# Recurrent scan and gated FFN on one core: one product for three parameters, one row spread earlier, and a new transfer order before the first down projection

## The chip, the cores and the metric

The kernel runs on one core of one Trainium2 chip. The metric is the device time of one execution in microseconds (us), as the median of repeated runs. In the profile, PE is TensorE (matmuls), PEld its weight loads, DVE is VectorE, ACT is ScalarE, POOL is GpSimd, and SP is SyncE, which issues nearly all transfers here. Times within an execution are counted from the start of the profiled span.

## What is computed

The input is x with 2048 positions of 512 features in bf16. It is normalised over the features, and two branches are built from the normalised xn:

```python
xn  = layernorm(x)
Bu  = xn @ B_bar.T                    # complex, B_bar = ((Lam_bar - 1) / Lam)[:, None] * B
h_t = Lam_bar * h_{t-1} + Bu_t        # complex, Lam_bar = exp(exp(log_dt) * Lam)
y   = 2 * real(h @ C.T) + xn * Dskip
g   = silu((gelu(xn @ w_gate) * (xn @ w_up)) @ w_down)
out = x + y * g
```

The parameters Lambda_re, Lambda_im and log_dt are vectors of 512; Dskip is a row of 512; B and C are complex 512 x 512; the FFN is 1376 wide.

## The kernel before

**Slabs.** The 2048 positions are worked in four slabs (0 to 3) of 512, each of four tiles `m` of 128 positions. For each slab, `gate_tile` (L519, products recorded at L530) multiplies the transposed xn with `w_gate` and `w_up`; ACT evicts the results as `gt` (gelu) and `ub` (L538, L546); DVE multiplies them into `at` (L548, L550); `at_t` (L553) turns `at` by a transposing transfer into `atT` (L556); `down_pair` (L563, matmuls at L573) multiplies it with `w_down` for two tiles, and ACT evicts silu as `g` (L577). Slab 0 uses `GatePair` (L479) in three column chunks instead (matmuls L501, evictions L513 for `ub` and L514 for `gt`, product L516), because weights and xn arrive piece by piece.

**Recurrence.** `inputs` (L628) forms B times xn for half of the state (L638, evicted as `U` at L641). `states` (L644) rotates it so that the complex recurrence becomes real scans: a product `Q` with the tables `tab` (L656), sums into `W` (L664), four scans into `Fs` (L675), a product `Q` again (L656) and sums into `hst` (L664). `y_tile` (L582, matmuls L601) multiplies `hst` with `C2` onto the skip term already in the bank; DVE multiplies with `g` (`yg`, L604), adds x (`ot`, L606), and the result is stored (L609).

**Preparation.** `columns` (L391) turns log_dt and Lambda_im from rows to columns by a matmul with an identity; `damping` (L736) does the same for Lambda_re in a second matmul (L739) with a copy (L740), and derives the damping `rho` on POOL. `head_t` (L744) transposes the centred x of slab 0 on PE (L445), and ACT or DVE evicts it (L448, L449). `spread` (L747) copies Dskip's row to all partitions with a one-row matmul (L748) and an eviction (L749). `tables` (L708) builds `tab` on DVE (L725). `coefficients` (L822) forms `cre`, `cim`, `ncre` in two groups of tiny DVE operations (L827 to L834, and L837 to L845). The transposed C (`CT`, which lies in the buffer `hst1`) becomes `C2` for each of four column groups: ACT forms `tF` (L897), and DVE forms two products from it (L899, L902). There is one `tF` buffer, so the next `tF` waits for both products of the one before.

**PSUM.** Three slots of two banks and two single banks. `slot()` hands the three slots round in turn; a product into a slot waits until ACT has evicted what was in it.

**What sets the order.** Every operation is added to a plan (`Plan`, L24) with an estimated cost, its reads and writes, and sometimes `after` (a forced predecessor), `rank` (a preference) or `not_before`. PE operations keep the order in which the code adds them; all other engines, and SP's queue of transfers, get the order that `run` (L154) finds by list scheduling and a random search. The order is fixed when the program is built. `dma_first` chains transfers on one queue. Slab 1's statistics and normalisation (`norm1`, L860) run on DVE; those of slabs 2 and 3 (`norm_act`, L871) load x and let ACT form sums by two passes over each tile (`junk`, L876).

Of the kernel before, what the change touches and what calls it, by code (L numbers as in the profile page):

```python
# [12 lines left out]
AF = mybir.ActivationFunctionType  # L13
# [189 lines left out]
def kernel(  # L203
# [17 lines left out]
    nc = tc.nc  # L221
    P = 128
# [27 lines left out]
    def sb(name, shape, dt=BF16):  # L250
        return consts.tile(shape, dt, name=name)
# [5 lines left out]
    wd = sb("wd", [P, NFT, D])  # L257
    BT = sb("BT", [P, 2, KT, D])
    C2 = sb("C2", [P, 2, NPT, D])
    pv = [sb("pv0", [2 * NPT, P]), sb("pv1", [NPT, P])]  # L260
    Drow = sb("Drow", [P, D])
    hst = [sb(f"hst{i}", [P, 2, NPT, TS]) for i in range(2)]
    CT = hst[1]
# [67 lines left out]
    def load_x(eng, q, m, land):  # L331
        dma_first(eng, 0.45, land, lambda: q.dma_start(out=x_tok[:, m, :], in_=x_r[:, m, :]), [("x", 0, m)], not_before=0.72)

    load_p(0, A_log_dt, pv[0][0:NPT, :])
    load_p(1, A_Lambda_im, pv[0][NPT : 2 * NPT, :])
    behind = [first[ACT]]
    load_p(2, A_Lambda_re, pv[1][:])
    dma(ACT, 0.4, 3.0, lambda: nc.scalar.dma_start(out=Drow[0:1, :], in_=A_Dskip.rearrange("(a d) -> a d", a=1)), writes=["Drow"], after=[first[ACT]], rank=-20.0)
    def load_first(c, which, land):
        load_w(dma_first, SP, nc.sync, c, (1.45 * (CH0[c][1] - CH0[c][0]) / 512, land), which)  # L340
# [10 lines left out]
    def load_rest():  # L351

        for ri, src in enumerate((A_B_re, A_B_im)):
            dma_first(SP, 1.9, 5.0, lambda ri=ri, src=src: nc.sync.dma_start_transpose(out=BT[:, ri, :, :], in_=src), [("BT", ri)])
        first[SP] = turn_slab(0, 3.5, [first[SP]])
        dma_first(SP, 1.45, 3.5, lambda: nc.sync.dma_start(out=x_tok[:, M : 2 * M, :], in_=x_r[:, M : 2 * M, :]), [("x", 1, m) for m in range(M)])
        for which in range(2):
            load_w(dma_first, SP, nc.sync, 2, (1.35, 3.5), which)
        load_c(0)

    def load_c(ri):
        dma_first(SP, 1.9, 4.0, lambda: nc.sync.dma_start_transpose(out=CT[:, ri, :, :], in_=(A_C_re, A_C_im)[ri]), [("CT", ri)])

    def turn_slab(s, land, after=()):

# [20 lines left out]
    acts(1, lambda: act(out=tiny[:], in_=zero[:], func=AF.Exp), ["zero"], ["tiny"], table="exp", rank=150.0, after=behind)  # L386
    pf = small("pf", 16)
    dt_, thn, lim, lre = (pf[:, 4 * i : 4 * i + 4] for i in range(4))
    rows = slots[2][:, 0, 0 : 2 * NPT]

    def columns():  # L391

        pe(1, 150, lambda: T.matmul(rows, lhsT=pv[0][:], rhs=ident[0 : 2 * NPT, 0 : 2 * NPT], start=True, stop=True),
            [("pv", 0), ("pv", 1), "ident"], [("slot", 2, 0)])
        acts(4, lambda: act(out=dt_, in_=rows[:, 0:NPT], func=AF.Exp), [("slot", 2, 0), "tiny"], ["dt"], table="exp", rank=150.0)

    def turn_angles():
        dve(4, lambda: V.tensor_copy(out=lim, in_=rows[:, NPT : 2 * NPT]), [("slot", 2, 0)], ["lim"], base=0.14)
        dve(4, lambda: V.tensor_tensor(out=thn, in0=lim, in1=dt_, op=ALU.mult), ["lim", "dt"], ["thn"])

    iota_i = sb("iota_i", [P, NBA], I32)
# [77 lines left out]
    class GatePair:  # L479
# [24 lines left out]
        def close(self):  # L504
            m, c, q, pss = self.m, self.c, self.q, self.pss
            a, b = CH0[c]
            w = b - a
            qb, qo = q // 2, (q % 2) * 512
            gd, ud = gt[qb][:, qo : qo + w], ub[qb][:, qo : qo + w]
            kw, rd, ptr = {}, [], 0  # L510
            if self.bare:
                kw, rd, ptr = dict(scale=rs[:, 0, m : m + 1]), [("rs", 0, m)], 1
            up = acts(w, lambda: act(out=ud, in_=pss[1][:, 0:w], func=AF.Copy, **kw), self.both + rd, [("ub", q)], ptr=ptr)  # L513
            gelu = acts(w, lambda: act(out=gd, in_=pss[0][:, 0:w], func=AF.Gelu_apprx_tanh, **kw), self.both + rd, [("gt", q)], table="gelu", ptr=ptr,  # L514
                 after=[*early, up] if c + m == 0 else (), rank=60.0 if c + m == 0 else 0.0)
            dve(w, lambda: V.tensor_tensor(out=at[m][:, a:b], in0=gd, in1=ud, op=ALU.mult), [("gt", q), ("ub", q)], [("at", m, c)], rate=2.0)  # L516
            return gelu

    def gate_tile(s, m):  # L519
# [24 lines left out]
        for kind, (nm, wt, dst) in enumerate((("wg", wg, gt[q]), ("wu", wu, ub[q]))):  # L544
# [5 lines left out]
        dve(b - a, lambda: V.tensor_tensor(out=at[j][:, a:b], in0=gt[q][:, a:b], in1=ub[q][:, a:b], op=ALU.mult),  # L550
            [("gtb", q), ("ubb", q)], [("at", j, 2)], rate=2.0)

    def at_t(s, m, c0, c1):  # L553
        j = (s * M + m) % NAT
        k0, k1 = CK[c0][0], CK[c1][1]
        dma(SP, 1.3, 2.2, lambda: nc.sync.dma_start_transpose(  # L556
            out=atT[:, k0:k1, m * P : (m + 1) * P], in_=at[j][:, k0 * P : k1 * P]),
            [("at", j, c) for c in range(c0, c1 + 1)] + [("atpad", j)], [("atT", m, c) for c in range(c0, c1 + 1)])

    g2s = {}  # L560
    g2_n = [0]
# [60 lines left out]
    def half(s, h):  # L622
        inputs(s, h)
        states(s, h)
# [76 lines left out]
        else:  # L701
            dve(196, lambda: V.scalar_tensor_tensor(out=kr[:], in0=ang[:], scalar=-1.0, in1=ang[:], op0=ALU.mult, op1=ALU.max), ["ang"], ["kr"], base=0.13)

    def sines():
        early.append(acts(196, lambda: act(out=sbt[:], in_=ang[:], func=AF.Sin, scale=TWO_PI), ["ang"], ["sbt"], table="silu", rank=20.0))
        early.append(acts(196, lambda: act(out=cbt[:], in_=kr[:], func=AF.Sin, scale=-TWO_PI, bias=halfpi[:]), ["kr", "halfpi"], ["cbt", "trig"], table="silu", rank=20.0))

    def tables(behind):  # L708
        NB4 = [P, NPT, NA, NB // 2, 2]
# [25 lines left out]

    def damping():  # L736

        ps = ybank[0][:, 0:NPT]
        pe(1, 150, lambda: T.matmul(ps, lhsT=pv[1][:], rhs=ident[0:NPT, 0:NPT], start=True, stop=True), [("pv", 2), "ident"], [("y", 0)])  # L739
        dve(4, lambda: V.tensor_copy(out=lre, in_=ps), [("y", 0)], ["lre"], base=0.14)  # L740
        dve(4, lambda: V.tensor_tensor(out=a1[:], in0=lre, in1=dt_, op=ALU.mult), ["lre", "dt"], ["a1"])
        power(rho[:], e_t[:], a1[:], 4, ["a1", "e_t"], ["rho"])

# [30 lines left out]
    norm_dve(0, 0)  # L774
    pl.in_turn = False
    head_t(0, ACT)
    dummies(2, 0)
    behind = [head_t(1, ACT)]
    acts(1, lambda: act(out=tiny[:], in_=zero[:], func=AF.Sin), ["zero", "dt"], ["tiny"], table="silu", rank=60.0, after=behind)
    sines()  # L780
    pairs = [GatePair(m, 0, m == M - 1) for m in range(M)]
    pairs[0].products(0)
    spread()
    pairs[1].products(0)
    pairs[0].products(1)
    head_t(2, ACT)
    pairs[1].products(1)
    damping()
    pairs[2].products(0)
    pl.in_turn = True  # L790
    head_t(3, DVE)
# [4 lines left out]
    pairs[2].products(1)  # L796
    pairs[3].products(0)
    pairs[3].products(1)
    gelus = [p.close() for p in pairs]
    tables(gelus[:1])  # L800
    load_rest()
# [2 lines left out]

    def gate_pairs(m, c):
        p = GatePair(m, c, (c, m) == (1, M - 1))
        p.products(0)
        p.products(1)
        p.close()

    for m in range(M):
        gate_pairs(m, 1)
    for h in range(2):
        half(0, h)
    for m in range(M):
        gate_pairs(m, 2)
        at_t(0, m, 0, 2)

    c1, s1 = cbt[:, :, 1], sbt[:, :, 1]
    cre, cim, ncre = small("cre"), small("cim"), small("ncre")  # L820
# [36 lines left out]
             [("x", s, m), ("rs", s, m), ("nb", s)], [("xn", m)], ptr=2)  # L857
        dma(SP, 1.2, 1.3, lambda: nc.sync.dma_start_transpose(out=xnT[s % 2][:, m, :, :], in_=xn[m]), [("xn", m)], [("xnT", s % 2, m)])

    def norm1():  # L860
        for m in range(M):
            stats(1, m)
            mean(1, m)
        rstd(1, 0, M)
        for m in range(M):
            norm_dve(1, m)
        first[SP] = turn_slab(1, 3.0, [first[SP]])
        for m in range(M):
            skip(1, m)

    def norm_act(s):  # L871
        dma(SP, 0.5, 4.0, lambda: nc.sync.dma_start(out=x_tok[:, s * M : (s + 1) * M, :], in_=x_r[:, s * M : (s + 1) * M, :]),
            writes=[("x", s, m) for m in range(M)], not_before=(30.0, 50.0)[s - 2], rank=40.0)
        for m in range(M):
            for i, fn in enumerate((AF.Copy, AF.Square)):
                acts(512, lambda i=i, fn=fn, m=m: act(out=junk[:], in_=x_tok[:, s * M + m, :], func=fn, accum_out=sx[:, s, i, m : m + 1]),  # L876
                     [("x", s, m)], ["junk", ("sx", s, i, m)], ptr=2)
        mean, var = sx[:, s, 0, :], sx[:, s, 1, :]

        def f():  # L880
            V.tensor_scalar(out=mean, in0=mean, scalar1=1.0 / D, scalar2=None, op0=ALU.mult)
            V.tensor_tensor(out=mq[:, s, :], in0=mean, in1=mean, op=ALU.mult)
            V.tensor_scalar(out=var, in0=var, scalar1=1.0 / D, scalar2=EPS, op0=ALU.mult, op1=ALU.add)
            V.tensor_tensor(out=var, in0=var, in1=mq[:, s, :], op=ALU.subtract)
        pl.add(DVE, 0.35, f, [("sx", s, i, m) for i in range(2) for m in range(M)], [("var", s)], lag=0.13)
        power(rs[:, s, :], var, mhalf[:], M, [("var", s), "mhalf"], [("rs", s, m) for m in range(M)])
        dve(M, lambda: V.scalar_tensor_tensor(out=nb[:, s, :], in0=mean, scalar=-1.0, in1=rs[:, s, :], op0=ALU.mult, op1=ALU.mult),
            [("var", s)] + [("rs", s, m) for m in range(M)], [("nb", s)])
        for m in range(M):
            norm_out(s, m)  # L890

    norm1()
    dma_first(SP, 3.6, 4.3, lambda: nc.sync.dma_start(out=wd[:, 0 : NFT - 1, :], in_=B_w_down[0 : (NFT - 1) * P, :].rearrange("(k p) d -> p k d", p=P)), ["wd"])
    dma_first(SP, 0.4, 4.3, lambda: nc.sync.dma_start(out=wd[:FL, NFT - 1, :], in_=B_w_down[(NFT - 1) * P : F, :]), ["wd"])
    load_c(1)
    for pt in range(NPT):
        acts(1024, lambda pt=pt: act(out=tF[:, :, :], in_=CT[:, :, pt, :], func=AF.Copy, scale=cim[:, pt : pt + 1]),  # L897
             ["coef", ("CT", 0), ("CT", 1)], [("tF",)], ptr=1)
# [67 lines left out]
```

## Time and profile before

| | us |
|---|---|
| time, median of 3 runs (180.31 to 180.37) | 180.33 |
| span of the profiled execution | 179.2 |
| PE busy | 172.7 |
| DVE busy | 157.7 |
| ACT busy | 119.2 |

The page gives busy time by engine, 40 equal slices of the span (4.48 us each) with the busy share in tenths, transfers, the chain of work that ended last, and the costliest groups of instructions. The trace behind it answers further: a timeline lists instructions by start time with, in brackets, how long the engine sat idle before and what ended that; the waits list sums up such idle times. A matmul's end in this trace is modelled, and matmuls overlap, so the distance from start to start is what counts: a 128x512 matmul of L638 has a mean duration of 379 ns in the page, while 32 of them in a row (from 32.44 to 39.34 us) start 0.216 us apart. On ACT and DVE, too, an instruction starts a little before the one ahead of it has ended.

### The profile page before, as it was taken

What the parts mean: (1) busy time and instruction counts of PE and PEld (TensorE: products, weight loads), DVE (VectorE), ACT (ScalarE), POOL (GpSimd) and SP (SyncE); (2) the same over time, 40 slices, a digit from 0 to 9 for tenths busy, and PEclk for the clock granted to TensorE, in tenths of its full rate; (3) what the DMA queues carried; (4) which work ended last, traced back from release to release, by engine and by line L of the source; (5) the groups of instructions that cost most, each with busy time, mean ns of one, the idle gap of its engine ahead of it and who ended that gap; (6) DMA issues with size and microseconds to landing.
All of it is one profiled execution on the core that took longest, in us unless ns stands there. A gap on an engine that the chain in (4) does not pass through costs nothing.

```text
span 179.2 us, 2387 instructions
## 1 busy us (share of the span) xinstructions
PE 172.7 (96%) x838; PEld 82.3 (46%) x852; DVE 157.7 (88%) x268; ACT 119.2 (67%) x180; POOL 8.0 (4%) x17
## 2 busy tenths in 40 slices
PE   7999999999899999999999999999999999999992
PEld 2454444444344445444445554544445555444451
DVE  3989899999999999999999999999999999860063
ACT  3899988669999998938249863554518666353220
POOL 2120022000002000000020000000000000000000
PEclk9999999999999999999999999999999999999998
DMA  5999997999500479500011575141100344420011
GB/s 145 317 252 216 311 99 155 348 251 221 134 0 0 80 139 117 107 29 2 0 59 33 104 139 104 40 80 33 60 0 0 71 83 93 95 73 29 0 58 59
DMA packets 49093, 18.53 MB, mean 103 GB/s; under 512 B 40409, under 2 KB 49082, under 8 KB 49082
## 3 DMA queue, kind: packets, MB, share of 16 engines
q1 hardware_dynamic: 49056, 18.39, 46.7%
q8 instruction: 6, 0.10, 0.3%
q14 instruction: 5, 0.04, 0.1%
q10 hardware_dynamic: 26, 0.00, 0.0%
HBM read 6.33 MB, written 2.10 MB: 47 GB/s over the span
## 4 chain that ended last, share of the span: by engine, by line
PE 69%; DVE 16%; DMA 8%; ACT 4%; issue 2%; DVEq 0%; SPq 0%
PE slot L530 30%; PE slot L573 17%; PE ybank L601 13%; PE slot L638 8%; DMA x_tok<-in_A_x_dram 4%; DMA atT<-at 3%; DVE Q L656 3%; DVE Fs L675 3%; DVE st L420 2%; DVE at L516 1%; DVE Q L725 1%; DMA out_dram<-ot 1%; DVE sk L473 1%; DVE ot L606 1%; DVE xn L461 1%
## 5 line engine op out<-in xcount | busy, mean ns | idle before, releaser
L530 PEld LDWEIGHTS <-xnT 128*128 128x128 bf16 x288 | 28.2, 98 | 28.4
L573 PE MATMUL slot<-wd,atT 128*128 128x512 bf16 (+1 forms) x172 | 38.7, 379 | 0.9 <-DMA atT<-at 0.7
L530 PE MATMUL slot<-wu,xnT 128*128 128x512 bf16 (+1 forms) x141 | 31.6, 356 | 0.3
L530 PE MATMUL slot<-wg,xnT 128*128 128x512 bf16 (+1 forms) x141 | 31.3, 356 | 0.1
L675 DVE TENSOR_TENSOR_SCAN Fs<-rho,ini,W 128x512 bf16<-128x512 f32 x24 | 29.4, 1270 | 0.1
L638 PE MATMUL slot<-xnT,BT 128*128 128x512 bf16 x128 | 28.6, 379 | 0.0
L601 PE MATMUL ybank<-C,hst 128*128 128x512 bf16 (+1 forms) x125 | 27.9, 372 | 0.2
L573 PEld LDWEIGHTS <-atT 128*128 128x128 bf16 (+1 forms) x176 | 17.1, 98 | 21.8 <-DMA atT<-at 1.2
L604 DVE TENSOR_TENSOR yg<-ybank,g 128x512 bf16<-128x512 f32 (+1 forms) x16 | 10.7, 670 | 12.7 <-PE ybank L601 12.6
L641 ACT ACTIVATE U<-slot 128x1024 bf16<-128x1024 f32 x16 | 16.0, 1018 | 8.0 <-PE slot L638 8.0
L577 ACT ACTIVATE g<-slot 128x1024 f32<-128x1024 f32 x8 | 8.2, 1024 | 17.3 <-PE slot L573 17.3
L601 PEld LDWEIGHTS <-hst 128*128 128x128 bf16 x136 | 13.3, 97 | 13.8
L638 PEld LDWEIGHTS <-BT 128*128 128x128 bf16 x128 | 12.5, 98 | 15.1
L656 DVE TENSOR_TENSOR Q<-U,tab 128x4096 bf16<-128x4096 bf16 x8 | 18.3, 2289 | 0.3
L656 DVE TENSOR_TENSOR Q<-Fs,tab 128x4096 bf16<-128x4096 bf16 x8 | 18.3, 2288 | 0.1
L538 ACT ACTIVATE gt<-slot 128x1024 bf16<-128x1024 f32 x12 | 12.3, 1024 | 7.0 <-PE slot L530 5.4
L597 ACT ACTIVATE ybank<-sk 128x512 f32<-128x512 bf16 (+1 forms) x16 | 9.3, 586 | 9.2 <-DVE yg L604 9.2
L538 ACT ACTIVATE ub<-slot 128x1024 bf16<-128x1024 f32 x12 | 12.3, 1024 | 3.2 <-PE slot L530 3.0
L876 ACT ACTIVATE junk<-x_tok 128x512 bf16<-128x512 bf16 x16 | 10.1, 629 | 2.3 <-DMA x_tok<-in_A_x_dram 2.1
L675 DVE TENSOR_TENSOR_SCAN Fs<-rho,W 128x512 bf16<-128x512 f32 x8 | 9.2, 1208 | 0.0
L501 PEld LDWEIGHTS <-W 128*128 128x128 bf16 x64 | 5.9, 98 | 5.5 <-DVE W L449 0.3
L548 DVE TENSOR_TENSOR at<-gt,ub 128x1024 bf16<-128x1024 bf16 x12 | 8.2, 684 | 0.2 <-ACT ub L538 0.2
(122 smaller groups left out, 182.3 us busy)
## 6 DMA issues: line engine op xcount, KB each, us to landing
out_dram<-ot SPq DMA_DIRECT2D x15, 128.0 KB, 1.7
x_tok<-in_A_x_dram SPq DMA_DIRECT2D x3, 512.0 KB, 6.5
wd<-in_B_w_down_dram SPq DMA_DIRECT2D x1, 1280.0 KB
x_tok<-in_A_x_dram SPq DMA_DIRECT2D x4, 128.0 KB, 2.7
wg<-in_B_w_gate_dram SPq DMA_DIRECT2D x1, 512.0 KB
wu<-in_B_w_up_dram SPq DMA_DIRECT2D x1, 512.0 KB, 6.5
wg<-in_B_w_gate_dram SPq DMA_DIRECT2D x1, 480.0 KB
wu<-in_B_w_up_dram SPq DMA_DIRECT2D x1, 480.0 KB, 6.4
```

The lines of the kernel that those rows point to most:

```text
L530: T.matmul(ps[:, bank, 0 : b - a], lhsT=xnT[s % 2][:, m, k, :], rhs=wt[:, k, a:b], start=(k == 0), stop=(k == KT - 1))
L538: acts(1024, lambda ps=ps, dst=dst, fn=fn: act(out=dst[:, 0:1024].rearrange("p (c w) -> p c w", c=2), in_=ps[:, :, :], func=fn), [("slot", ...
L548: dve(1024, lambda: V.tensor_tensor(out=at[j][:, 0:1024], in0=gt[q][:, 0:1024], in1=ub[q][:, 0:1024], op=ALU.mult), qs[0] + qs[1], [("at", ...
L573: T.matmul(ps[:, b, :], lhsT=atT[:fs, k, m * P : (m + 1) * P], rhs=wd[:fs, k, :], start=(k == 0), stop=(k == NFT - 1))
L597: acts(w, lambda: act(out=bank, in_=sk[s % 2][:, m, a:z], func=AF.Copy), [("sk", s % 2, m)], [key])
L601: T.matmul(bank, lhsT=hst[s % 2][:, j // NPT, j % NPT, m * P : (m + 1) * P], rhs=C2[:, j // NPT, j % NPT, a:z], start=False, stop=(j == 2 ...
L604: dve(w, lambda: V.tensor_tensor(out=yg[e][:, a:z], in0=bank, in1=g2[gi][:, b, a:z], op=ALU.mult), [key, ("g2", gi)], [("yg", e, a)], base ...
L638: T.matmul(ps[:, ri, :], lhsT=BT[:, ri, k, pt * P : (pt + 1) * P], rhs=xnT[s % 2][:, :, k, :], start=(k == 0), stop=(k == KT - 1))
L641: acts(1024, lambda q=q, ps=ps: act(out=U[ui][:, :, q, :], in_=ps[:, :, :], func=AF.Copy), [("slot", i, 0), ("slot", i, 1)], [("U", ui, q)])
L656: dve(4096, lambda: V.tensor_tensor(out=Qf, in0=src.unsqueeze(1).to_broadcast(WQ), in1=table, op=ALU.mult), reads, ["Q"], rate=2.0)
L675: pl.add(DVE, 1.116 if s == 0 else 1.19, lambda ri=ri, q=q, pt=pt, first=first: V.tensor_tensor_scan(out=Fs[:, ri, q, :], data0=rho[:, pt ...
L876: acts(512, lambda i=i, fn=fn, m=m: act(out=junk[:], in_=x_tok[:, s * M + m, :], func=fn, accum_out=sx[:, s, i, m : m + 1]), [("x", s, m)] ...
```

## The change

It has six parts.

1. log_dt, Lambda_im and Lambda_re go into one tile `pv` of 12 rows and are turned by one product; one DVE copy takes the last two, and `damping` loses its matmul and its copy.
2. `spread` moves from behind the first gate product to between the first two transpositions, in place of one of two warming matmuls.
3. Both halves of C are transposed in `load_rest`, ahead of slab 1's transposition. Before, the second half could be placed anywhere behind the load of `wd`.
4. The transposing transfers of `at` get a fixed order; the load of x for slab 2 is forced directly behind slab 0's first one.
5. In `GatePair`, each eviction waits only for its own bank, and the first pair of the second chunk computes its up product first.
6. `sines` is forced behind the third head transposition; `norm1` and the `wd` load stand earlier in the code, `damping` later.

```diff
@@ tiles and parameters
-    pv = [sb("pv0", [2 * NPT, P]), sb("pv1", [NPT, P])]
+    pv = sb("pv", [3 * NPT, P])
...
-        pe(1, 150, lambda: T.matmul(rows, lhsT=pv[0][:], rhs=ident[0 : 2 * NPT, 0 : 2 * NPT], start=True, stop=True),
-            [("pv", 0), ("pv", 1), "ident"], [("slot", 2, 0)])
+        pe(1, 150, lambda: T.matmul(rows, lhsT=pv[:], rhs=ident[0 : 3 * NPT, 0 : 3 * NPT], start=True, stop=True),
+            [("pv", 0), ("pv", 1), ("pv", 2), "ident"], [("slot", 2, 0)])
...
-        dve(4, lambda: V.tensor_copy(out=lim, in_=rows[:, NPT : 2 * NPT]), [("slot", 2, 0)], ["lim"], base=0.14)
+        dve(8, lambda: V.tensor_copy(out=pf[:, 2 * NPT :], in_=rows[:, NPT:]), [("slot", 2, 0)], ["lim", "lre"], base=0.14)
@@ def damping
-        ps = ybank[0][:, 0:NPT]
-        pe(1, 150, lambda: T.matmul(ps, lhsT=pv[1][:], rhs=ident[0:NPT, 0:NPT], start=True, stop=True), [("pv", 2), "ident"], [("y", 0)])
-        dve(4, lambda: V.tensor_copy(out=lre, in_=ps), [("y", 0)], ["lre"], base=0.14)
@@ def load_rest
-        load_c(0)
+        for ri, src in enumerate((A_C_re, A_C_im)):
+            dma_first(SP, 1.9, 4.5, lambda ri=ri, src=src: nc.sync.dma_start_transpose(out=CT[:, ri, :, :], in_=src), [("CT", ri)])
@@ class GatePair, close
-            up = acts(w, ..., self.both + rd, [("ub", q)], ptr=ptr)
-            gelu = acts(w, ..., self.both + rd, [("gt", q)], table="gelu", ptr=ptr,
+            up = acts(w, ..., self.both[1:] + rd, [("ub", q)], ptr=ptr)
+            gelu = acts(w, ..., self.both[:1] + rd, [("gt", q)], table="gelu", ptr=ptr,
@@ def at_t
-        dma(SP, 1.3, 2.2, lambda: nc.sync.dma_start_transpose(
+        turned[s, m] = dma(SP, 1.3, 2.2, lambda: nc.sync.dma_start_transpose(
...
+            after=[turned[s, m - 1]] if m else [first[SP]] if s == 0 else [])
@@ order of the first products
     head_t(0, ACT)
-    dummies(2, 0)
+    dummies(1, 0)
+    spread()
     behind = [head_t(1, ACT)]
...
-    sines()
     pairs = [GatePair(m, 0, m == M - 1) for m in range(M)]
     pairs[0].products(0)
-    spread()
     pairs[1].products(0)
     pairs[0].products(1)
-    head_t(2, ACT)
+    sines([head_t(2, ACT)])
     pairs[1].products(1)
-    damping()
...
     pairs[3].products(1)
+    damping()
@@ gate_pairs and slab 0's third chunk
+        up_first = (c, m) == (1, 0)
+        p.products(up_first)
+        p.products(not up_first)
...
     for m in range(M):
         gate_pairs(m, 2)
         at_t(0, m, 0, 2)
+        if m == 0:
+            turned[0, 0] = load_slab(2, [turned[0, 0]])
@@ def norm_act
-        dma(SP, 0.5, 4.0, ... load of x of slab s, rank=40.0)
+        if s > 2:
+            load_slab(s)
...
-    load_c(1)
```

## The prediction

> **What bounds the kernel now.** I read the page first. PE is busy in 172.7 of 179.2 us, and apart from the first and last slices every slice is full.
>
> ```profile
> PE 172.7 (96%) x838; PEld 82.3 (46%) x852; DVE 157.7 (88%) x268; ACT 119.2 (67%) x180; POOL 8.0 (4%) x17
> PE   7999999999899999999999999999999999999992
> ```
>
> So a change can gain only where PE stands still, and costs whatever new standstill it makes. The list of waits for PE has three entries:
>
> ```profile
> PE slot L437 <- DVE zero L381: 1.1, 1, 1.1
> PE slot L573 <- DMA atT<-at: 0.7, 1, 0.7
> PE ybank L445 <- DVE Fs L466: 0.4, 1, 0.4
> ```
>
> The first is the start and the third the second head transposition; the second is slab 0's down projection waiting for its last transposed tile. Matmul ends are modelled, so I measure from start to start: the stall before 47.37 us is about 0.9 us, and no other from 13 us to the end is as large. SP's queue shows why that tile is late (columns: start, duration, queue, line, operation):
>
> ```profile
> 29.52 0.69 SPq L872 DMA_DIRECT2D x_tok<-in_A_x_dram  x1
> 31.76 7.78 SPq L556 DMA_TRANSPOSE atT<-at  x3
> 39.59 2.23 SPq L362 DMA_TRANSPOSE hst<-in_A_C_im_dram  x1
> 41.91 1.82 SPq L556 DMA_TRANSPOSE atT<-at  x1
> ```
>
> C's second transposition stands between the third and the fourth tile. The fourth took 5.41 us from issue to landing (chain of waits) and landed at 47.32.
>
> What becomes critical when this goes is on ACT and DVE. The timeline there:
>
> ```profile
> 20.59 1.29 DVE L420 BATCH_NORM_STATS2 st<-x_tok 128x6 f32<-128x512 bf16 x2 [0.76 <-DMA x_tok<-in_A_x_dram]
> ...
> 37.46 0.63 ACT L876 ACTIVATE junk<-x_tok 128x512 bf16<-128x512 bf16 x1 [2.07 <-DMA x_tok<-in_A_x_dram]
> ...
> 46.48 0.75 DVE L902 SCALAR_TENSOR_TENSOR C<-hst,ncre,tF 128x512 bf16<-128x512 bf16 x1
> 47.15 4.57 DVE L675 TENSOR_TENSOR_SCAN Fs<-rho,W 128x512 bf16<-128x512 f32 x4
> ...
> 49.16 1.14 ACT L897 ACTIVATE tF<-hst,cim 128x1024 f32<-128x1024 bf16 x1
> 50.20 1.01 ACT L577 ACTIVATE g<-slot 128x1024 f32<-128x1024 f32 x1
> 51.23 1.28 ACT L538 ACT_TABLE_LOAD   x1
> 52.52 1.02 ACT L538 ACTIVATE gt<-slot 128x1024 bf16<-128x1024 f32 x1
> 54.41 1.89 PE L530 MATMUL slot<-wg,xnT 128*128 128x512 bf16 x8
> ```
>
> Read it from below. PE's second gate tile of slab 1 starts at 54.41 in the slot that `gt` frees at 53.54. There is 0.8 us of slack, but `gt` comes behind a table load, the second `g`, and the second `tF`, with no gap between them.
>
> [...] ACT stood 2.07 us before the `junk` at 37.46. [...] x of slab 2, issued 2.2 us ahead of the first `at` transposition, landed first (7.9 us after issue, at 37.4; the transposition 6.9 after, at 38.7). [...] `gt` starts 1.31 us after `g` ends[...]. I use 1.29 from start to start.
>
> **Part by part.** I set the built order of the changed kernel on each engine beside that of before. PE's order changes only at the beginning.
>
> *One product, spread, sines, damping: 0.* Lambda_re lands at 3.58 us by the landing records, Dskip's row at 4.17; PE reached `columns` at 3.73 and will reach `spread` near 4.9, so neither waits. The spread left behind and damping's matmul (0.38 and 0.16 us) lie where PE waits for ACT's evictions anyway (ends 6.53 and 9.13, next products 6.79 and 9.27). The third eviction hangs on the second table load, `tiny` and the spread's eviction in either order. The fourth hangs on the DVE chain that reaches 10.77; one tiny operation joins it and one copy leaves it. Bounds: 0.2 us less to 0.1 more.
>
> *Own bank per eviction, up first: +0.15.* ACT now takes three `gt` before the `ub`. At 0.46 us from start to start from 12.38, the second pair's `ub` is fifth and ends near 14.83; PE wants that bank at 14.73. It ends in the next item's slack.
>
> *C ahead, fixed queue: -0.9 of stall.* C's second half takes 2.2 us of issue behind its first, which ends at 23.05, so by 25.3. Slab 1's transposition waits for its xn until 26.5 anyway, landed 4.4 us after issue, and is wanted at 32.2: slack of about 1 us. The fourth `at` product is ready earlier too (behind two scans instead of four). Its transfer should land by 43 to 45, against 46.4 wanted. The stall goes.
>
> *What the new order puts in its place: +1.2.* The DVE now does the first eight tiny coefficient operations ahead of the tables and meets the wait for slab 1's x (20.59, unchanged, since the queue up to there is) with one table product (1.14) more still to do. And ACT has a third `tF` ahead of the second `g`. It needs the second pair of C2 products, which stands behind the first scan of the second half. Sum for DVE, from before: the first pair ended at 47.23. To come: 1.14 (table product), 1.13 (scan), 1.32 (second pair). To go: 0.58 (eight tiny operations, now before 20.59) and 0.12 (`a`). That is 50.12; two dependent neighbours now without work between them add some 0.07 each, so 50.25 (50.1 to 50.4). Then on ACT: wait 0.05, `tF` 1.04, `g` 1.03, load 1.29, `gt` 1.02 to its end: 54.68. PE 0.06 later: 54.74. Before: 54.41. Effect +0.33 us.
>
> *x of slab 2 behind the first `at` transposition.* ACT's chain has a second gate, its landing X. From X to the end of `gt`: `junk` 3 x 0.75 + 0.62, `tF` 1.04, `U` 0.90, `junk` 0.62, `U` 0.90, `junk` 0.75 + 0.62, `tF` 1.15, load 1.29, `g` 0.93, `tF` 1.04, `g` 1.03, load 1.29, `gt` 1.02 = 15.45. X was 37.4. Now it has one transposition of `at` ahead of it (about 1.2 us, the distance from the first landing to the second, 38.7 to 40.0): 38.6, and between 37.9 and 39.7, since issuing that transposition took between 1.8 and 3.9 us. 38.6 + 15.45 = 54.05, under 54.68: DVE sets the end while X is below 39.2. The same X frees the slot of the second down pair at X + 4.9 = 43.5; PE wants it at 44.05. From 39.1 a stall opens there too. Queued behind these waits is all of ACT, hence each of PE's slots.
>
> From 54.4 on PE has no gap in the profile of before and the same work in the same order, so the difference goes through to the end. I looked for new ones: slab 0's first `y` needs `hst` and C2, near 62 now, wanted at 63.9 or later; x of slab 2 normalised by 68, wanted at 73.7. The tail is the same.
>
> Sum: -0.9 (stall) + 1.23 (new stalls at 52 to 55, which take in the 0.15) = +0.33, so 180.33 + 0.33 = 180.7.
>
> **Rivals.** *A: the stall goes and nothing replaces it.* Speaks for it: 0.8 us of slack at 54.41, and idle ACT (67% busy). Against: the third `tF` cannot start before 50.1. Time: 180.33 - 0.9 = 179.4, faster. *B: the late x or the earlier C costs more.* If X is 39.7, `gt` ends at 55.15, and the time is 181.1; if slab 1's transposition lands 1.5 us later, 0.5 us of stall is added at 32.2, but ends in the same slack. For it: the DMA queues are full from 31 to 46 us (share of about 1.0 in every 2 us window). Against: 37.4 was reached behind 1.28 MB of `wd`. *C: it comes out even.* DVE gains 0.2 to 0.3 somewhere, for instance in the start: 180.4.
>
> **Numbers.** Forecast 0.50, at 180.7; A 0.15; B 0.20, at 181.1; C 0.15. The forecast's centre, +0.33, lies near the edge of 0.2% (0.36 us, so 180.69): I give it half above and half below. Slower 0.25 + 0.20 and a little for unknown costs, 0.48; same 0.25 + 0.12 = 0.37; faster 0.15. Range: B's upper end 181.1 and 0.1 for its size, 181.2; below, C and a part of A, 179.8.
>
> **What would show it.** Right: no wait of PE for `atT`; C's second half issued right behind the first; `tF` three times before the second `g`, the third near 50.3 with a wait for DVE; a new wait of PE L530's counterpart for ACT near 54.7, and a smaller one near 52.4; slab 2's x landing near 38.6. Wrong: a `gt` that ends by 53.4, or DVE reaching the second C2 pair before 49, would make it A; an x landing after 39.2 makes it B.

## The result and the profile after

The changed kernel took 182.85 us (median of four, 182.81 to 182.92), beside 180.32 (180.27 to 180.37) for the kernel before: a ratio of 1.0141, with a 95% interval of 1.0123 to 1.0158. It is 2.5 us slower. The forecast of 180.7 and its range up to 181.2 were too low. Executions of one kernel differ by up to 2.3 us on one chip (180.0 to 182.3 for the kernel before), so what follows compares medians beside the kernel before on the same chip, and stages of one trace with the same stages of another.

The page of the changed kernel, first the busy times, then PE's row of the forty slices:

```profile
PE 175.1 (97%) x836; PEld 83.3 (46%) x850; DVE 157.5 (87%) x267; ACT 119.8 (66%) x180; POOL 9.2 (5%) x17
PE   7998999999999999999999999999999999999992
```

PE has two matmuls fewer than before and is busy 2.4 us longer. So the loss is not only in waits: some matmuls took longer. PE's waits, by engine, line and releaser:

```profile
PE slot L436 <- DVE zero L380: 1.1, 1, 1.1
PE slot L500 <- ACT ub L512: 0.7, 1, 0.7
```

The wait for `atT` is gone, as forecast. In its place is one for ACT's `ub` in the second chunk of slab 0, and none near 55 us.

The trace's records of when PE starts its products, from start to start, give where the time went. "First chunk done" is the start of the second chunk's first product, "second chunk done" that of the first product of B with slab 0, which follows it.

| PE starts, us | first gate product | first chunk done | second chunk done | down projection | first `y` | last matmul |
|---|---|---|---|---|---|---|
| before | 5.73 | 12.14 | 19.05 | 39.34 | 63.70 | 175.41 |
| after | 6.18 | 14.05 | 21.78 | 42.07 | 65.61 | 177.32 |
| difference | +0.45 | +1.91 | +2.73 | +2.73 | +1.91 | +1.91 |

Three steps make it: 1.9 in the first 14 us, 0.8 in the second chunk, and 0.8 given back around the place where before waited for `atT`. From there to the end the two traces run in parallel. The traces differ by 1.9 and the times by 2.5; the rest is in the kernel before, whose profiled execution took 181.0, 0.67 more than its timed runs (more on this below).

**The start.** PE's part of the timeline, before:

```profile
3.85 0.40 PE L437 MATMUL slot<-junk 128*128 128x512 bf16 x1
4.29 0.40 PE L445 MATMUL ybank<-ident,Fs 128*128 128x128 bf16 x4
4.52 0.59 PE L437 MATMUL slot<-junk 128*128 128x512 bf16 x2
5.50 0.40 PE L445 MATMUL ybank<-ident,Fs 128*128 128x128 bf16 x4 [0.38 <-DVE Fs L466]
5.73 0.81 PE L501 MATMUL slot<-wg,W 128*128 128x384 bf16 x4
```

and after:

```profile
3.85 0.61 PE L436 MATMUL slot<-junk 128*128 128x512 bf16 x1
4.25 0.63 PE L444 MATMUL ybank<-ident,Fs 128*128 128x128 bf16 x4
4.67 0.63 PE L436 MATMUL slot<-junk 128*128 128x512 bf16 x1
5.24 0.60 PE L747 MATMUL slot<-Drow,junk 1*128 1x512 bf16 x1
5.78 0.61 PE L444 MATMUL ybank<-ident,Fs 128*128 128x128 bf16 x4
6.18 2.76 PE L500 MATMUL slot<-wg,W 128*128 128x384 bf16 x8
8.74 1.45 PE L500 MATMUL slot<-wu,W 128*128 128x384 bf16 x4
```

Eight products of 384 columns fill the 2.56 us from 6.18 to 8.74, 0.32 us each; before, such products start 0.165 us apart. The records of PE's clock say why: full rate began at 3.91 us before and at 10.02 after. The page's clock row has 9 in the first slices of both; it does not show this. Twelve products at twice the duration are 1.9 us more. PE was already 0.45 late at the first of them, and the spread, which no longer stands among them, gives 0.4 back, so the sum is again 1.9.

**The second chunk.** The timeline of ACT and PE, after:

```profile
14.91 1.89 PE L500 MATMUL slot<-wg,W 128*128 128x512 bf16 x8
...
15.68 0.59 ACT L512 ACTIVATE ub<-slot,rs 128x384 bf16<-128x384 f32 x1
16.84 0.58 ACT L512 ACTIVATE ub<-slot,rs 128x384 bf16<-128x384 f32 x1 [0.56 <-PE slot L500]
17.47 1.02 PE L500 MATMUL slot<-wu,W 128*128 128x512 bf16 x4 [0.67 <-ACT ub L512]
```

Read the two waits together. PE's up product of the second tile needs the bank that `ub` frees at 17.42. But that `ub` itself stood 0.56 us, waiting for PE: for the gate product that PE had just put into the other bank of the same slot (started at 15.77; the product in its own bank had started at 10.25). The plan now has each eviction depend on its own bank, and so puts the gate product ahead of the `ub`; the wait that the instruction carries is still one for the slot. From start to start PE loses 0.83 us.

**The queue and ACT later on.** SP's queue, after:

```profile
17.81 6.09 SPq L361 DMA_TRANSPOSE hst<-in_A_C_re_dram  x1
23.95 1.93 SPq L361 DMA_TRANSPOSE hst<-in_A_C_im_dram  x1
27.77 1.99 SPq L365 DMA_TRANSPOSE xnT<-xn  x1
...
32.88 2.77 SPq L557 DMA_TRANSPOSE atT<-at  x1
35.69 0.58 SPq L830 DMA_DIRECT2D x_tok<-in_A_x_dram  x1
36.37 6.23 SPq L557 DMA_TRANSPOSE atT<-at  x3
```

C's second half is issued behind its first, and slab 1's transposition landed at 32.13, where PE came to it at 35.17. Slab 2's x was issued only when the first transposition of `at` had left the queue. The timeline of ACT, with one line of DVE, and PE's product behind it:

```profile
40.58 0.63 ACT L885 ACTIVATE junk<-x_tok 128x512 bf16<-128x512 bf16 x1 [0.74 <-DMA x_tok<-in_A_x_dram]
...
50.75 1.02 ACT L579 ACTIVATE g<-slot 128x1024 f32<-128x1024 f32 x1
51.03 0.74 DVE L904 SCALAR_TENSOR_TENSOR C<-hst,cre,tF 128x512 bf16<-128x512 bf16 x1
...
51.87 1.15 ACT L902 ACTIVATE tF<-hst,cim 128x1024 f32<-128x1024 bf16 x1
52.93 1.00 ACT L579 ACTIVATE g<-slot 128x1024 f32<-128x1024 f32 x1
53.95 1.28 ACT L537 ACT_TABLE_LOAD   x1
55.24 1.02 ACT L537 ACTIVATE gt<-slot 128x1024 bf16<-128x1024 f32 x1
56.32 1.89 PE L529 MATMUL slot<-wg,xnT 128*128 128x512 bf16 x8
```

x landed at 40.6 and `gt` ended at 56.26, far behind the forecast's 38.6 and 54.68. PE starts at 56.32 with less than 0.1 us of wait only because it was 1.8 us late itself. So the late start hides a second loss.

Two things hold `gt` here. ACT works without a pause from the landing of x, except for 0.2 us ahead of the third `tF` at 51.87. That `tF` waited for DVE's second pair of C2 products, whose last ended at 51.77, as the prediction had it.

### The profile page after: what moved, and what is told of

It is laid out like the page before. It is cut to its first block, busy times and chain, and to the rows that moved or that the text cites. A ratio compares the mean times of both kernels' runs of the same rounds, so it can differ in the third digit from the quotient of the medians.

```text
span 181.1 us, 2382 instructions
## 1 busy us (share of the span) xinstructions
PE 175.1 (97%) x836; PEld 83.3 (46%) x850; DVE 157.5 (87%) x267; ACT 119.8 (66%) x180; POOL 9.2 (5%) x17
## 4 chain that ended last, share of the span: by engine, by line
PE 93%; DMA 2%; DVE 1%; ACT 1%; issue 1%; DVEq 0%; ACTq 0%
PE slot L529 29%; PE slot L575 21%; PE slot L640 15%; PE ybank L603 13%; PE slot L500 10%; PE slot L436 2%; PE ybank L500 2%; DMA xnT<-xn 1%; DMA out_dram<-ot 1%; PE ybank L444 1%; DVE ot L608 1%; DVE yg L606 1%; ACT gt L537 1%; ACT ub L512 0%; PE slot L747 0%
## 5 line engine op out<-in xcount | busy, mean ns | idle before, releaser
L640 PEld LDWEIGHTS <-BT 128*128 128x128 bf16 x128 | 12.5, 98 | 15.1
L500 PEld LDWEIGHTS <-W 128*128 128x128 bf16 x64 | 6.6, 107 | 7.8 <-issue 2.5
```

Of the source, the lines that this page charges most:

```text
L500: T.matmul(ps[:, 0 : b - a], lhsT=src[:, m, k, :], rhs=wt[:, k, a:b], start=(k == 0), stop=(k == KT - 1))
L640: T.matmul(ps[:, ri, :], lhsT=BT[:, ri, k, pt * P : (pt + 1) * P], rhs=xnT[s % 2][:, :, k, :], start=(k == 0), stop=(k == KT - 1))
```

## The experiments

Theory F: the loss has three parts, PE's half rate at the start, the slot's wait in the second chunk, and slab 2's late x. In the first runs F stands for the first part alone: what PE did early decides when full rate begins. The rivals are named with each run.

### The kernel before, again

Nothing edited; it gives the spread.

> The kernel before, unchanged, for a second profile. The profile of before shows matmuls at half rate up to 3.9 us and full rate from there; the profile of the changed kernel shows half rate up to 10.0 us, although both kernels give PE the same work up to 3.7 us. Theory F (what PE did early decides[...]): full rate again from the first 4 us, time 180.3. Theory G (the moment is a matter of chance from run to run): the moment moves to anywhere between 3 and 10 us, and the time with it, up to 182.

Median 180.87 (180.07 to 181.82), beside 180.83 of the other runs of before. In its trace PE was at full rate from 4.19 us, and the wait for `atT` at 47.47 was there, 1.06 us from start to start, in an execution of 181.1.

### The changed kernel with one more full warming product

```diff
-    dummies(1, 0)
+    dummies(1, 0, more=1)
     spread()
```

> The changed kernel with one more full warming matmul between the first head transposition and the spread; nothing else moves. Theory F: full rate by about 6.6 us instead of 10.0, the first gate products end some 1.5 us earlier, time 181 to 181.5. Theory G, or a cause that has nothing to do with these matmuls: still 10.0 us and 182.9, or a little more for the added matmul (0.4).

Median 181.88 beside 180.83, ratio 1.0081 (1.0005 to 1.0156). Full rate came at 4.53 us, just before the two warming products, one of them the added one, that start from 4.61, and the profiled execution took 182.12; 181 to 181.5 had been expected. The stall in the second chunk stayed (0.84 us), and a new one showed: PE's second gate tile of slab 1 waited for `gt`, at 55.53, 1.15 us from start to start. So with a fast start the changed kernel still loses.

### The kernel before with one warming product of one row

```diff
-    dummies(2, 0)
+    dummies(2, 0, rows=(P, 1))
```

> The kernel before with the second of its two warming matmuls after the first head transposition cut to one row (same columns, same time on PE, like the spread matmul that stands there in the changed kernel); order and data otherwise the same. Theory F: full rate only from about 10 us[...], time about 182; no change where full rate comes before that matmul, as it did in the profile of before (3.9 us). Theory G: no connection, 180.3.

At full rate a product of one row takes 0.38 us (the spread at 6.48 in the trace of before), as the full one does, and nothing depends on it. Twelve of 17 executions took 180.05 to 181.03, five 182.41 to 183.25; the kernel before had none above 181.61 in 28. The median hardly moved (180.92, ratio 1.0025, 0.9997 to 1.0052), but a second group about 1.9 us up appeared. The profile is of one of the twelve: full rate came at 5.44, 0.2 us after the one-row product had begun.

### The kernel before with both warming products of one row

```diff
-    dummies(2, 0)
+    dummies(2, 0, rows=(1, 1))
```

> The kernel before with both warming products after its first head transposition cut from 128 rows to one; they take the same time and no other work depends on them. Theory F: with one of them cut, 5 of 17 executions took 1.9 us longer than the rest; with both, at least half are, so the median is 182.0 to 183.0, and the profile, if it catches one, shows full rate only near 9 to 11 us. Rival P: the times of before, median within 0.3 of it, at most 1 in 10 above 182.

Twelve of 19 took 180.08 to 181.05 and seven 181.93 to 182.67; the kernel before had none above 181.4 in 32. I had expected at least half. So the one-row products do push executions into a group 1.9 us up, the size of the half-rate start, but the share (5 of 17, 7 of 19) hardly rises with the second. No profile caught one of this group. This one is early (180.08 us): full rate at 4.18, before the first one-row product at 4.60. It shows something else, with the order of before on every engine:

```profile
30.98 7.54 SPq L557 DMA_TRANSPOSE atT<-at  x3
38.57 2.17 SPq L362 DMA_TRANSPOSE hst<-in_A_C_im_dram  x1
40.83 1.58 SPq L557 DMA_TRANSPOSE atT<-at  x1
...
39.33 9.68 PE L574 MATMUL slot<-wd,atT 128*128 128x512 bf16 x43
```

PE runs through slab 0's down projection without a wait. SP's queue reached the fourth transposition 1.1 us earlier than in the profile of before, and the stall for `atT` is not there. In the profiles of before and its variants near 181.0 it is there, in this one at 180.08 it is not.

### The changed kernel again, and with a spread of 128 rows

```diff
-T.matmul(slots[2][:, 1, :], lhsT=warm[0:1, 0:P], rhs=Drow[0:1, :], ...)
+T.matmul(slots[2][:, 1, :], lhsT=warm[:, 0:P], rhs=Drow[:, :], ...)
```

`Drow` is set to zero first. The product is in the same place and takes 0.39 us at full rate (below), beside 0.38 with one row in the run with the extra product.

> The changed kernel, nothing edited, on another occasion. Theory F (the cost has two parts: PE at half rate until about 10 us in executions[...], and two stalls that are always there, at 15 to 18 and near 55 us): times fall into two groups, 181.4 to 182.2 and 182.6 to 183.4, and a profile in which PE is at full rate by 5.5 us shows a wait of PE for ACT of 0.7 us or more near 55.5. Rival G (the late full rate belongs to the program, not to chance): all times between 182.6 and 183.4.

> The changed kernel, but the product that spreads D's row reads 128 rows instead of one (127 of them zero), in the same place and for the same time; the order on every engine is the same except for one more small memset on DVE. Theory F[...]: full rate by 5.6 us, no execution above 182.4, median near 181.7. Rival G (the rows do not matter; the place of the spread or the later products do): times like the changed kernel's, with executions of 182.6 to 183.3, and full rate only near 10 us in them.

Then both once more, on another chip:

> The changed kernel, nothing edited, on a third occasion. Theory F[...]: times in two groups, around 181.8 and around 183.0; the profile shows either full rate by 5.6 us with a wait for ACT near 55, or full rate near 10 us without it. Rival P (half rate until 10 us comes by chance in all these kernels alike): the same share of executions above 182.6 in the kernel with the spread of 128 rows.

> The changed kernel with a spread of 128 rows, once more, beside the changed kernel. Theory F: no execution above 182.5, full rate by 5.6 us, a median at least 0.3 below that of the changed kernel. Rival P: medians within 0.2, and the same share of late ones.

One row: 182.47 (181.6 to 183.09) and 182.51 (181.42 to 182.94), beside 180.46 of before both times. 128 rows: 182.18 (181.71 to 182.38) and 182.30 (181.52 to 183.35). PE's start with 128 rows, first occasion:

```profile
4.97 0.39 PE L747 MATMUL slot<-Drow,junk 128*128 128x512 bf16 x1
5.54 0.40 PE L444 MATMUL ybank<-ident,Fs 128*128 128x128 bf16 x4 [0.18 <-DVE Fs L465]
5.78 1.68 PE L500 MATMUL slot<-wg,W 128*128 128x384 bf16 x8
```

The traces go with theory F: full rate at 10.02, 10.41 and 9.56 us in the three profiles with one row, at 4.53, 4.32 and 3.71 in the three with a full product there. But they can't show it. In the three early ones full rate came before the added or widened product had started (4.61 at the earliest, 4.97 and 4.70), and up to there PE had done the same work as in the late ones. So what sets these profiles apart is not the edit, and no record shows what it is.

That leaves the times, and they agree only in part. The median with 128 rows had been expected near 181.7 the first time and at least 0.3 below the changed kernel the second time; it was 0.29 and 0.21 below, and the second occasion had two executions above 182.5. Over all occasions, 10 of 16 executions of the changed kernel took 182.6 or more, and 3 of 16 of those with a full product (the run with the extra product and the two with 128 rows). So the counts suggest that the one-row product makes late starts more frequent. It is not all of the loss: with a full one the kernel is still 1.05 (the extra product), 1.7 and 1.8 us (128 rows) behind before. Nor does every long execution need one: with 128 rows and x ahead (below), 5 of 22 took 182.0 to 182.5 beside a median of 181.05, and the kernel before itself took more than 182 in 3 of 143. No profile caught any of these.

What remains is in the chain of waits of the first 128-row run (start, duration, what):

```profile
34.69 4.87 DMA x_tok<-in_A_x_dram
39.56 0.02 issue
39.58 0.73 ACT junk L885 x2
...
50.68 1.14 ACT tF L902
51.82 0.91 ACT g L579
52.75 1.28 ACT L537
54.03 0.01 issue
54.04 1.03 ACT gt L537
55.08 0.04 issue
55.12 2.97 PE slot L529 x13
```

From the landing of x at 39.56 to `gt`, ACT never stops: 15.5 us. PE waits for its end, 0.87 us from start to start. The third `tF` at 50.68 waits for nothing; DVE had its second pair of C2 products done at 50.46. So x sets the end here, but DVE is close behind: where the third `tF` did wait for DVE, it started 0.09 after that pair, which would be 50.55. With an x landing earlier and nothing else changed, the end could come only some 0.1 us sooner (estimate from these figures). On the second occasion it was the same: `tF` at 50.91, the pair done at 50.71, and a wait of PE of 1.15 us. The stall in the second chunk was 0.84 both times.

### Both evictions wait for both banks

```diff
-self.both[1:] + rd, [("ub", q)]      # and self.both[:1] for gt
+self.both + rd, [("ub", q)]
-        up_first = (c, m) == (1, 0)
+        up_first = False
```

> The changed kernel with the evictions of slab 0 depending on both banks of their slot again, and the gate product first in the second chunk; the plan is made anew with that. The changed kernel has one stall of PE of 0.8 us at 17.5 us, on the up eviction of the second pair, which itself waited for the next gate product into the other bank of the same slot. Theory H (planning by bank while the wait is by slot makes this stall): the stall at 17.5 is gone, time 0.5 to 0.8 us less, about 182.1 to 182.4. Rival (the late start of the products alone makes it): the stall stays, 182.8.

Median 181.78 of three (180.84 to 182.28). The profiled execution got full rate only at 10.28 us, yet the second chunk took 6.99 us, where it took 7.73 in the changed kernel and 6.91 before: the stall there is gone.

Then the same with the old head as well (two warming products, the spread behind the first gate product):

> The changed kernel with two of its parts undone: the head has its second full warming product and the spread behind the first gate product again, and both evictions of a pair wait for both banks, gate first. The scheduler then puts the third tF behind the first gt of slab 1. Theory F: full rate by 5.5 us, no wait of PE near 17.5, no wait for ACT near 55 above 0.3 us, no wait for atT: 0.7 to 1.0 faster than the kernel before, about 180.0 when that is at 180.8. Rival H (the queue order behind slab 0's gate products costs in itself, by the late x of slab 2): 180.6 to 181.4, with a wait of PE for ACT between 43 and 55 us.

Median 180.99 beside 180.46, ratio 1.0021 (1.0004 to 1.0037); on the same chip the changed kernel had 182.47. Full rate at 4.04, first chunk done at 11.99, second chunk at 18.89, both 0.15 ahead of before, no wait for `atT`. But PE waits 1.15 us for `gt` at 54.51, with x landed at 39.2; the third `tF` stands behind this `gt` here, so it cannot be what holds it. Theory F missed this one: it had expected that gate to go with the order of `tF`. Rival H, the late x, holds: with `tF` out of the chain, x makes the wait by itself.

### C ahead alone, and C ahead with a fixed order

```diff
-        load_c(0)
+        load_c(0); load_c(1)
```

(and the later `load_c(1)` away).

> The kernel before, with C's second transposition issued directly behind its first, ahead of slab 1's; nothing else is edited. The scheduler keeps ACT's second g and the first gt of slab 1 ahead of the third tF here, and slab 2's x ahead of slab 0's gate products on SP's queue. Theory: the wait for atT near 47.4 goes and nothing replaces it, slab 1's transposition lands before 32.2: 0.9 faster than before, about 179.9 when before is at 180.8. Rival H (with C ahead a wait for ACT or for slab 1's transposition takes the place, as forecast in the step on the new order): no gain, 180.6 to 181.0.

It came out at 182.59 beside 180.46, ratio 1.0125 (1.0085 to 1.0166): neither theory had this.

```profile
32.41 8.34 SPq L556 DMA_TRANSPOSE atT<-at  x4
...
41.44 9.69 PE L573 MATMUL slot<-wd,atT 128*128 128x512 bf16 x43 [1.93 <-DMA atT<-at]
```

The built order shows why: without C between them, the scheduler issues the transposition of the first tile third. PE needs it first, at 39.34; it was issued at 37.62 and landed at 41.39. The fixed order of the change is what C ahead needs. With that order alone added, and x still ahead of the first `at`:

```diff
+            after=[turned[s, m - 1]] if m and s == 0 else [])
```

> The kernel before, with C's second transposition directly behind its first, and slab 0's four transpositions of gate products in the order of their tiles; slab 2's x stays ahead of them on SP's queue, which the changed kernel does not do. Theory X (C ahead needs the fixed order, and it is slab 2's x behind the first gate product that costs in the changed kernel): no wait of PE for atT, none for ACT near 55 us, x of slab 2 landed by 38.3, PE 0.7 to 0.9 earlier than before from 48 us to the end; the median faster than before by as much as the stall had in ordinary executions, 0.3 to 0.9. Rival H (C ahead pushes back slab 1's transposition or x in any order): a new wait near 32 or 55 us, and no gain.

> The kernel before with C ahead and slab 0's transpositions in the order of their tiles, slab 2's x ahead of them, on a second chip (first: 0.9977, 0.9963 to 0.9990, with no gap of PE from 6 us to the end). Theory X: 0.3 to 0.5 faster than before by the medians, and no execution above 181.0. Rival: within 0.2 of before, since the stall for atT is absent from ordinary executions.

Medians 180.33 beside 180.74 and 180.14 beside 180.46: ratios 0.9977 (0.9963 to 0.9990) and 0.9982 (0.9969 to 0.9994). It beats both kernels, by 0.3 to 0.4 us. In the first trace x had landed at 37.7, the third `tF` stands behind `gt` as in before, and PE runs without a gap where the two kernels have theirs:

```profile
39.44 9.68 PE L574 MATMUL slot<-wd,atT 128*128 128x512 bf16 x44
48.96 1.89 PE L530 MATMUL slot<-wg,xnT 128*128 128x512 bf16 x8
...
53.60 1.89 PE L530 MATMUL slot<-wg,xnT 128*128 128x512 bf16 x8
```

Its last matmul starts at 174.61, 0.8 before the one in the profile of before; its fastest executions (180.01, 179.96) are no faster than those of before (180.0, 179.98). That fits a stall that only some executions of before have.

### x ahead of the first gate product

```diff
+    first[SP] = load_slab(2, [first[SP]])
     for m in range(M):
         gate_pairs(m, 2)
         at_t(0, m, 0, 2)
-        if m == 0:
-            turned[0, 0] = load_slab(2, [turned[0, 0]])
```

On the kernel with the 128-row spread:

> The changed kernel with the spread of 128 rows (so that PE is at full rate by 5.6 us) and with slab 2's x issued ahead of slab 0's first gate product instead of behind it. Compared with the same kernel with x behind it (median 182.2, a wait of PE for ACT of 0.87 at 55.1): theory X (the late x sets ACT's chain) has x landed by 38.3, no wait for ACT above 0.2 near 55, and 0.7 to 0.9 less. Rival D (DVE's second pair of C2 products sets it, as forecast): the wait stays at 0.5 or more wherever the third tF stands ahead of gt, and the time stays within 0.3. The stall of 0.8 near 15.5 us stays in both.

On the one with the old head and both banks:

> The kernel with the old head and both evictions of a pair waiting for both banks (measured at 181.0 beside 180.5 of before, with a wait of PE for ACT of 1.15 at 54.5), and now also with slab 2's x ahead of slab 0's first gate product. Theory X: x landed by 38.3, none of the stalls at 15.5, 47 and 55 us; 0.8 to 1.1 less than without the edit, so 180.0 beside 180.5 of before, or faster. Rival D (DVE sets it): the third tF stands ahead of the first gt of slab 1 here, so the wait near 55 stays above 0.5.

Both were run on a chip where before took 180.74. The first: 181.05, ratio 1.0029 (1.0011 to 1.0047), against 1.0085 without the edit. The second: 181.09, ratio 1.0023 (1.0001 to 1.0046), against 1.0021: nothing gained. x landed 1.1 to 1.3 us sooner (38.3 and 38.1), and the wait near 55 went in the first and fell from 1.15 to 0.44 in the second. But both have a new wait for ACT (PE's timeline, first kernel):

```profile
40.72 9.67 PE L575 MATMUL slot<-wd,atT 128*128 128x512 bf16 x44 [0.85 <-ACT U L643]
```

With x planned earlier the scheduler put two of its statistics ahead of ACT's second eviction of `U`, and they stood 2.5 us waiting for x to land. The edit moves the loss from 55 to 40.7 us. The plan of the first kernel also lost the stall in the second chunk (0.47 at 12.5 instead) and put the third `tF` behind `gt`, so its gain cannot be put down to x alone. In the second the third `tF` stayed ahead of `gt` and started at 51.63, again 0.09 after DVE's pair. So rival D, that DVE sets the end, is not ruled out by these two.

### Own bank alone, on the kernel before

```diff
-self.both + rd, [("ub", q)]          # and self.both[:1] for gt
+self.both[1:] + rd, [("ub", q)]
-        p.products(0)
-        p.products(1)
+        u = (c, m) == (1, 0); p.products(u)
+        p.products(not u)
```

> The kernel before with one part of the change alone: each of slab 0's evictions waits for its own bank only, and the up product goes first in the first pair of the second chunk. Theory F: a wait of PE for ub of 0.7 to 0.9 from start to start in the second chunk, near 15.5 us, while the evicting instruction itself waits for PE; from there to 47 us PE is 0.8 later, the wait for atT at 47.4 shrinks by as much, so that the end is 0.0 to 0.5 later than before. Rival (the step as forecast, 0.15 that ends in slack): no wait above 0.2 near 15.5, the end within 0.2.

Median 183.53 beside 180.74, ratio 1.0147 (1.0117 to 1.0178), and not for either theory's reason. The second chunk has no stall (6.97 us). PE's waits:

```profile
PE slot L573 <- ACT U L641: 1.2, 1, 1.2
...
PE slot L530 <- ACT gt L538: 1.0, 1, 1.0
PE slot L530 <- ACT g L577: 0.4, 1, 0.4
```

Here too two statistics of x stand ahead of `U`, and ACT then waits 2.40 us for C's second half. So own-bank dependences need not stall: they let the scheduler choose another order, good or bad. As a test of that part alone the run is inconclusive.

## Why the prediction was wrong, step by step

**"One product, spread, sines, damping: 0"** failed, and it is the largest term. I priced the two moved products by their duration and found that they lie where PE waits anyway. I did not ask what their place did for PE's clock. By the clock records full rate lasted from 3.91 to 177.99 us in the trace of before and from 10.02 to 180.68 in that of the changed kernel. What PE does up to 3.7 us is the same in both, and PE's records, whose ends are modelled, leave no gap from 1.05 to 3.90 in either, so this work alone does not set the moment. In the changed kernel they leave none from 3.90 to 10.02 either, at half rate (products of 384 columns 0.32 us apart). The change takes one full warming product out of this stretch and puts the one-row product in, at 5.24.

The measured price is 1.7 to 2.1 us: the first chunk was done at 13.82, 14.05 and 14.26 in the three profiles of the changed kernel, and at 12.14 before. With a full product there, it was done at 12.06 and 11.93, so the rest of the step was right. That a one-row product in place of a full one lengthens a share of the executions by 1.9 us is shown by the two runs on the kernel before (12 of 36, against none of 60 on the same two chips). That these are late starts is argued from the size and from the changed kernel's traces; how the row count acts on the clock, no trace shows.

**"Own bank per eviction, up first: +0.15"** had the right place and a wrong size: 0.83. I took the `ub` as fifth in ACT's queue and its wait as that of its own bank. What it waited for was the slot, so it stood behind a gate product that was itself issued because the banks had been told apart.

**"-0.9 of stall"**: the stall went, and slab 1's transposition landed in time. But 0.9 was the stall of the profiled execution of before, at 181.0, and I took it from a time of 180.33. The trace at 180.08, of a variant with the same order, has no such stall. Taken out by itself, with the rest of the order kept, it is worth 0.3 to 0.4 on the medians.

**"What the new order puts in its place: +1.2"**: right in kind and near in size. With PE at full rate early, the wait for `gt` came at 55.1 to 55.5, forecast 54.74, and cost 0.87 to 1.15. The third `tF` did come third, at 50.7 to 51.1, forecast 50.3. In the profile with the extra product and in the three of the changed kernel it started 0.09 after DVE's second pair, so DVE held it as forecast, for 0.1 to 0.5 us. In the two 128-row profiles ACT came to it 0.2 after that pair, and x set the end by some 0.1.

**"x of slab 2 behind the first `at` transposition"** was mis-sized. The wait came 0.4 to 0.8 later than forecast because both gates did: DVE's second pair ended at 50.46 to 50.99, forecast 50.25, and x landed late. The chain of 15.45 us from the landing to the end of `gt` held: 15.5 measured. The landing did not: 38.6 forecast; 39.2, 39.6, 39.8 and 39.9 measured with an early start, 40.6 in the changed kernel. I had added the distance between two landings, 1.2 us. What x waits for is the issue of that transposition, which held SP's queue for 2.77 us (and began only when DVE had made the `at` tile), and then 4.9 us to its landing. My own limit for rival B was 39.2, so the rival's mechanism was at work, together with the forecast's: which of the two gates ends last changes from profile to profile.

The sum by traces with an early full rate: start -0.1, second chunk +0.8, `atT` -0.9, `gt` +0.9 gives +0.7 for the first 128-row run (its last matmul starts at 176.12, before's at 175.41) and +0.95 for the second, where I had +0.33. The late start adds 1.9 and hides the wait of 0.9 to 1.15 near 55, which makes the changed kernel's +1.9. To each comes what the profiled execution of before lies above its timed runs; that most of this is the stall is likely, not shown. For the changed kernel that is 1.91 + 0.67 = 2.58, measured 2.52. For the two 128-row runs, beside 180.46 (0.54 below 181.0), it is 1.2 and 1.5, measured 1.7 and 1.8: some 0.3 to 0.5 stays unaccounted.

## What to carry to other kernels

Ask of each part what a profile of one execution cannot answer: a stall that the profiled execution shows, in a time that is higher than the median, is not the stall of the median. A product that fills PE at the start is part of the schedule even where PE waits: thinning one or two such products to one row made 12 of 36 executions some 1.9 us longer, against none of 60. When full rate begins (3.91 and 10.02 us in the two traces) hardly shows in the busy share (96% and 97%) and not at all in the page's clock row; the distance between equal matmuls in the first 10 us shows it (0.165 and 0.32 us). Ask also whether a clock that is already up when the changed instruction starts can tell anything about that instruction. And a single part of such a change can be worse than the whole, as C ahead was without its fixed order: test the pair.

## What the runs showed of the hardware

The clock records of the two kernels' traces each have one stretch at full rate: from 3.91 to 177.99 us before and from 10.02 to 180.68 in the changed kernel, past PE's last matmul (which started at 175.41 and 177.32). Equal products of 384 columns start 0.165 us apart in it and 0.32 ahead of it.

PE's first product starts at 1.05 us in both. In 14 of the 18 profiles full rate came at 3.7 to 5.4 us. In the other four it came at 9.6 to 10.4 us: the changed kernel three times and the one with both banks, all with one warming product and the one-row spread between the head transpositions. What sets the moment, no trace shows. No trace caught a late start with a full product in place of the one-row one.

A matmul of one row took 0.38 us at full rate, like one of 128 rows (0.38 to 0.39). In its place it made 12 of 36 executions of the kernel before some 1.9 us longer, against none of 60. Why the rows should matter there, why no other program was caught with a late start, and whether the place of the spread matters beside its rows, stays open.
